# A gated pair of 2-D spectral filters on one core: folded transforms, 32-row inverse tiles, column 0 by a permutation matmul, the exchange through DRAM, last sums on GpSimd

## The chip, the cores and the metric

One core of one Trainium2 chip. The metric is the device time of one execution in microseconds, as the median of several. The profile covers one execution. Its span (first to last instruction) is 1.7 to 2.7 us shorter than the time of the same run. A run counts as slow when it is over 1.5% above the fastest of its kernel; verdicts use the others, the fast ones.

Some terms. In the views PE is TensorE's matmuls, PEld its weight loads, DVE is VectorE, ACT ScalarE, POOL GpSimd, and SP the queue of SyncE, which issues transfers. Matmuls write to the memory PSUM, and an eviction is the copy of a finished tile from there to the memory SBUF, where the next matmul reads it. The granted clock is PE's clock as a share of full speed. The DMA share is the mean busy share of the core's 16 DMA engines. A line such as L275 is a line of kernel.py. "Start to start" is the time from the start of one instruction to the start of the next on the same engine.

## The reference

```python
x = A_x                                     # (1, 2048, 1024) bf16
g = sigmoid((x * gate_w).sum(-1, keepdims=True))
a = irfft2(rfft2(x) * (A_w_r + 1j * A_w_i)) # over S = 2048 and D = 1024
b = irfft2(rfft2(x) * (B_w_r + 1j * B_w_i))
return g * a + (1 - g) * b
```

Both filters see the same x, so the forward transform is shared. The products differ, and the gate mixes the two on the way back.

## The kernel before

All transforms are matmuls with constant matrices. Row s is split as s2 (128) x s1 (16). A forward pass runs over s2 (`f1`), over d (`f2`) and over s1 (`f3`); then comes the complex product with both weights (`cmul`); the inverse runs over s1 (`i1`), over s2 with the gate's mix (`i2`) and over d (`i3`). Even and odd frequencies of d are separate ("par"). Each has 8 units of 256 rows, so 16 units in all. Between `i1` and `i2` the rows must change places, which is the exchange.

```python
def f2(n):                                   # over d: contraction of 512, output 512
    for tt in range(2):
        for q in range(4):
            nc.tensor.matmul(ps[:, tt*512:(tt+1)*512], lhsT=y[:, q, par, 2*t:2*t+2],
                             rhs=FD[:, par, q, :], start=(q == 0), stop=(q == 3))
    nc.scalar.copy(out=T, in_=ps)            # every eviction of the units is on ScalarE
...
def cmul(n):                                 # four products and two sums, all on DVE
    for r in range(2):
        nc.vector.tensor_tensor(p[r], xb[r], w, ALU.mult)       # 2048 elements
    nc.vector.tensor_tensor(Y[:, 0], p1[..., 0], p2[..., 1], ALU.subtract)   # 1024
    nc.vector.tensor_tensor(Y[:, 1], p1[..., 1], p2[..., 0], ALU.add)
...
def i1(n, r):                                # 64 x 64 tiles, two accumulating matmuls
    for k in range(2):
        for tt in range(2):
            for jh in range(2):
                nc.tensor.matmul(ps[hp(jh), tt*512:(tt+1)*512], lhsT=WI[hp(jh ^ tt), 2*u+tt, w, :],
                                 rhs=Y[hp(jh ^ tt), k, 2*tt:2*tt+2, o:o+256], ...)
    nc.scalar.copy(out=rl[:, :, r, :], in_=ps)
    if r == 1:                               # the exchange, SBUF to SBUF
        nc.gpsimd.dma_start(RR[par][p0:p0+29:4, :, :], rl[:, tt])
...
def gate_hat():                              # row sums of the gate, then turned by a DMA
    nc.scalar.copy(out=zs, in_=ps)           # (patterns cut) it writes single elements 16 apart
    nc.scalar.dma_start(zt, zs[0:97:32])
...
def i3(par, v):                              # over d, back: 4 matmuls of 512 columns per row
    for ch in range(4):
        nc.tensor.matmul(ps[:, s*512:(s+1)*512], lhsT=V[:, s, ch, :], rhs=IG[:, par*4+ch, :], ...)
    # even: copied to SBUF; odd: out = even + odd, even - odd, on DVE
```

## Time and profile before

| | before |
|---|---|
| time, median (range) | 146.72 us (146.09 to 148.42) |
| profiled span | 144.4 us |
| mean granted clock of PE | 0.96 |
| DMA traffic | 29.2 MB |

The first line of the profile's page gives busy time of each engine, its share of the span and its instructions:

```profile
PE 121.9 (84%) x1188; PEld 68.1 (47%) x1206; DVE 97.6 (68%) x113; ACT 93.3 (65%) x97; POOL 19.6 (14%) x37
```

No engine fills the span. The views by stage, which the prediction reads, show why: the bound moves from PE to ScalarE (ACT) and back. To read this kernel, use start-to-start intervals rather than printed durations, since neighbours overlap.

### The profile page before, as it was taken

To read this page: it belongs to the slowest core of one execution; us is meant where nothing else is said; L and a number is where in the kernel's file an instruction comes from. 1 tells how busy PE (TensorE), PEld (TensorE's weight loads), DVE (VectorE), ACT (ScalarE), POOL (GpSimd) and SP (SyncE) were. 2 spreads that over 40 slices of the span, in tenths; PEclk is the share of its full clock that TensorE was granted. 3 is DMA by queue.
4 is the path that set the end of the run, shared out by engine and by line. 5 is a ranking of instruction groups with operands and counts; after the bars stand their busy time and mean duration, and the time that the engine had idled before them with its cause. 6 is when DMAs were issued, how large, how long until landed. Compare 5 with 4: busy or idle time off the path is not lost.

```text
span 144.4 us, 2878 instructions
## 1 busy us (share of the span) xinstructions
PE 121.9 (84%) x1188; PEld 68.1 (47%) x1206; DVE 97.6 (68%) x113; ACT 93.3 (65%) x97; POOL 19.6 (14%) x37
## 2 busy tenths in 40 slices
PE   6999979929899898888867999868869999999910
PEld 2688844416344443334324345433455665756500
DVE  0177740089279999999999279599433456898990
ACT  4255546665699999999995899997935244253200
POOL 1000000000033222233333033033330000000000
PEclk9999999975799999999999999999999999999985
DMA  4999999968716999999865315527464000464553
GB/s 148 298 361 419 406 411 405 415 244 284 297 14 168 240 279 278 353 250 202 163 139 133 126 18 140 131 43 168 110 166 110 0 0 0 167 253 166 208 228 145
DMA packets 11088, 29.19 MB, mean 202 GB/s; under 512 B 3781, under 2 KB 4165, under 8 KB 10949
## 3 DMA queue, kind: packets, MB, share of 16 engines
q1 hardware_dynamic: 6048, 20.55, 38.3%
q0 software_dynamic: 4608, 8.41, 24.8%
q8 instruction: 9, 0.15, 0.5%
q10 hardware_dynamic: 420, 0.07, 0.3%
q14 instruction: 3, 0.02, 0.0%
HBM read 16.42 MB, written 4.19 MB: 143 GB/s over the span
## 4 chain that ended last, share of the span: by engine, by line
PE 55%; ACT 24%; DMA 9%; issue 4%; DVE 2%; another core or an unknown queue 2%; DVEq 1%; POOL 0%; ACTq 0%; POOLq 0%
PE pt L378 18%; PE pt L218 10%; PE pt L275 10%; ACT rl L349 10%; PE pv L367 9%; DMA re<-rl 5%; DMA zt<-zs 4%; ACT X L310 4%; ACT T L279 3%; PE pt L344 3%; ACT V L370 2%; PE pt L155 2%; ACT zs L245 2%; DVE ot L390 2%
## 5 line engine op out<-in xcount | busy, mean ns | idle before, releaser
L275 PE MATMUL pt<-fd,y 128*128 128x512 bf16 x117 | 30.5, 394 | 3.8 <-ACT rl L349 2.6
L349 ACT CAST rl<-pt 128x1024 bf16<-128x1024 f32 x32 | 32.9, 1038 | 0.0
L378 PE MATMUL pt<-ig,V 128*128 128x512 bf16 x121 | 29.6, 379 | 1.1 <-ACT V L370 0.7
L370 ACT CAST V<-pv 128x1024 bf16<-128x1024 f32 x16 | 16.3, 1021 | 19.2 <-PE pv L367 19.2
L344 PE MATMUL pt<-Y,wi 64*64 64x512 bf16 x256 | 20.1, 387 | 3.8 <-ACT T L279 0.8
L275 PEld LDWEIGHTS <-y 128*128 128x128 bf16 x128 | 12.6, 100 | 20.3 <-issue 8.6
L279 ACT CAST T<-pt 128x1024 bf16<-128x1024 f32 x16 | 16.3, 1017 | 8.3 <-PE pt L275 4.1
L378 PEld LDWEIGHTS <-V 128*128 128x128 bf16 x128 | 11.7, 98 | 13.9 <-ACT V L370 1.9
L354 POOL DMA_DIRECT2D re<-rl x16 | 9.6, 606 | 59.8 <-ACT rl L349 59.8
L310 ACT CAST X<-pt 128x1024 bf16<-128x1024 f32 x16 | 16.5, 1033 | 0.0
L218 PE MATMUL pt<-f_84,re 128*128 128x256 bf16 x128 | 15.6, 289 | 0.0
L218 PEld LDWEIGHTS <-re 128*128 128x128 bf16 x128 | 13.0, 103 | 3.1 <-DMA re<-in_x_dram 0.8
L228 ACT CAST y<-pt 128x1024 bf16<-128x1024 f32 x8 | 8.1, 1013 | 8.4 <-PE pt L218 8.4
L354 POOL DMA_DIRECT2D ro<-rl x16 | 9.5, 596 | 26.4 <-ACT rl L349 26.4
L386 DVE COPY re<-pt 128x1024 f32<-128x1024 f32 x5 | 6.1, 1225 | 10.2 <-PE pt L378 10.2
L226 DVE CAST y<-pt 128x1024 bf16<-128x1024 f32 x7 | 8.6, 1225 | 5.2 <-PE pt L218 5.2
L344 PEld LDWEIGHTS <-wi 64*64 64x64 bf16 x256 | 6.4, 106 | 11.9 <-issue 10.7
L389 DVE TENSOR_TENSOR ot<-pt,re 128x1024 bf16<-128x1024 f32 x8 | 9.8, 1224 | 3.0 <-PE pt L378 3.0
L367 PE MATMUL pv<-ea,re 128*128 128x128 bf16 x64 | 8.1, 219 | 2.9 <-DMA re<-rl 1.7
L295 PE MATMUL pt<-T,wf 64*64 64x512 bf16 (+2 forms) x192 | 9.8, 307 | 0.4 <-ACT T L279 0.3
L367 PEld LDWEIGHTS <-re 128*128 128x128 bf16 x128 | 7.5, 98 | 5.4 <-issue 2.5
L390 DVE TENSOR_TENSOR ot<-re,pt 128x1024 bf16<-128x1024 f32 x8 | 9.7, 1210 | 0.0
(96 smaller groups left out, 128.2 us busy)
## 6 DMA issues: line engine op xcount, KB each, us to landing
re<-rl POOLq DMA_DIRECT2D x16, 256.0 KB, 8.0
ro<-rl POOLq DMA_DIRECT2D x16, 256.0 KB, 5.1
out_dram<-ot SPq DMA_DIRECT2D x8, 512.0 KB, 2.6
re<-in_x_dram SPq DMA_DIRECT2D x7, 512.0 KB, 8.6
ro<-in_we_dram SPq DMA_DIRECT2D x4, 516.0 KB, 8.0
y<-in_wo_dram SPq DMA_DIRECT2D x4, 512.0 KB, 6.5
fd<-cst_fd SPq DMA_DIRECT2D x2, 512.0 KB, 9.1
ig<-cst_ig SPq DMA_DIRECT2D x1, 1024.0 KB
```

The source lines that it names most:

```text
L218: nc.tensor.matmul(ps[:, q * 256:(q + 1) * 256], lhsT=x[:, s1, h * 512 + q * 128:h * 512 + (q + 1) * 128], rhs=(bc(F1[:, 0, :]).to_broadca ...
L275: nc.tensor.matmul(ps[:, tt * 512:(tt + 1) * 512], lhsT=y[:, q, par, 2 * t:2 * t + 2, :, :].rearrange("p j s c -> p (j s c)"), rhs=FD[:, p ...
L279: nc.scalar.copy(out=T[:].rearrange("p a b -> p (a b)"), in_=ps[:])
L295: nc.tensor.matmul(ps[ho, tt * 512 + dst:tt * 512 + dst + ln], lhsT=WF[hp(jh), 2 * u + tt, w, :], rhs=T[hp(jh), tt, src:src + ln], start=( ...
L310: nc.scalar.copy(out=xo, in_=ps[:].rearrange("p (t r m) -> p t r m", t=2, r=2))
L344: nc.tensor.matmul(ps[hp(jh), tt * 512:(tt + 1) * 512], lhsT=WI[hin, 2 * u + tt, w, :], rhs=Y[hin, k, 2 * tt:2 * tt + 2, o:o + 256], start ...
L349: nc.scalar.copy(out=rl[:, :, r, :], in_=ps[:].rearrange("p (t m) -> p t m", t=2))
L354: nc.gpsimd.dma_start(RR[par][p0:p0 + 29:4, :, :], rl[:, tt].rearrange("p r m -> p (r m)"))
L367: nc.tensor.matmul(ps[:, s * 512 + ch * 128:s * 512 + ch * 128 + 128], lhsT=RR[par][:, s1, c0 + 256 * ab:c0 + 256 * ab + 128], rhs=Ew[:, s ...
L370: nc.scalar.copy(out=V[:].rearrange("p s c k -> p (s c k)"), in_=ps[:])
L378: nc.tensor.matmul(ps[:, s * 512:(s + 1) * 512], lhsT=V[:, s, ch, :], rhs=IG[:, par * 4 + ch, :], start=(ch == 0), stop=(ch == 3))
L390: nc.vector.tensor_tensor(ot[:, :, 1, :], ev, pv, ALU.subtract)
```

## The change

Nearly everything is rewritten to the same mathematics. The intent is to take work from PE and DVE at once.

- d is reordered on the host so that an element and its mirror are added and subtracted right after `f1`. A cosine half then needs only the sums, a sine half only the differences. `f2` has half the columns, and so has part of `i3`.
- `i1` uses 32-row tiles and accumulates all four products in PSUM, so the two DVE sums of `cmul` go.
- Column 0 (and 512), whose two real spectra share one complex column, are split by a permutation matmul and a small DVE patch.
- The exchange goes through DRAM.
- The gate is turned by one-row matmuls.
- GpSimd takes a part of the fold and of the last sums.
- A long list of tokens fixes the order of all engines, on eight single PSUM banks. A token is a step's name with its arguments, and the engine as D, P or A where there is a choice. `U` and `C` are the last stage for one row with 512 and with 256 columns (`i3`, `i3f`), `E` and `EX` copy its result, `EQ` adds the halves of an even row, `OR`, `QD` and `QP` are sums of odd rows, `Y`, `NA` and `N` treat column 0, `GT` and `GK` turn the gate.

```diff
 def f2(n, tt, k):
-        for q in range(4):
-            nc.tensor.matmul(ps[:, tt * 512:(tt + 1) * 512], ... rhs=FD[:, par, q, :], ...)
+        for v in range(2):
+            for b in range(2):
+                nc.tensor.matmul(ps[:, v * 256:v * 256 + 256], ... rhs=C["FD"][:, par, v, b, :], ...)
...
+    def fold(e, s1, par, a, b):
+        for v, op in enumerate((ALU.add, ALU.subtract)):
+            Q[e].tensor_tensor(yo[:, v, k:k + n, s1, :], a..., b..., op)
...
-        nc.vector.tensor_tensor(Y[:, 0, :, 0:M], p1[:, :, 0, 0:M], p2[:, :, 1, 0:M], ALU.subtract)
-        nc.vector.tensor_tensor(Y[:, 1, :, 0:M], p1[:, :, 1, 0:M], p2[:, :, 0, 0:M], ALU.add)
...
+        for q, (w, ri, wi) in enumerate(((0, 0, 0), (64, 1, 1), (128, 0, 1), (128, 1, 0))):
+            for tt in range(2):
+                for H in range(2):
+                    for j in range(2):
+                        r = slice(64 * H + 32 * j, 64 * H + 32 * j + 32)
+                        nc.tensor.matmul(o, lhsT=C["WJ"][r, 2 * u + tt, w:w + 64], rhs=src[r, ri, wi, tt],
+                                         start=(q == 0), stop=(q == 3))
...
-                nc.gpsimd.dma_start(RR[par][p0:p0 + 29:4, :, :], rl[:, tt]...)
+        Q[q].dma_start(SC[n // NU][a:a + 2].rearrange("a p m -> p a m"), RLs[n][:, tt])
+        Q[q].dma_start((Re, Ro)[par][:, v * 2048:v * 2048 + 2048],
+                       SC[par][:].rearrange("a (h v q) m -> (a h) v (q m)", h=4, v=8)[:, v])
...
-        nc.scalar.dma_start(zt[:], zs[0:97:32].rearrange("p t c s -> p (t c s)"))
+                nc.tensor.matmul(ps[32 * j:32 * j + 32, s1:s1 + 1], lhsT=TM["zs"][r, s1, :], rhs=C["one"][r, :], ...)
...
+            rh = bc(g[:, 0:256]).to_broadcast([P, 2, 256]) if ch < 2 else g[:, 256:768]   # i3: 512 columns, no sums
+            nc.tensor.matmul(ps[:, o:o + 256], lhsT=..., rhs=g[:, o:o + 256], ...)        # i3f: 256 columns, sums later
...
+        Q[e].tensor_tensor(EV[:, v, s, 256 * h:256 * h + 256], t[:, 0], t[:, 1], (ALU.add, ALU.subtract)[h])
```

## The prediction

> **What bounds the kernel now.** I read the page's header first: PE is busy 84% of the span, DVE 68%, ACT 65%, so no engine explains the time alone. So I cut the span into stages and asked for each engine's busy time in each. The columns are the stretch in us and its length, then busy us of each engine with its number of instructions, the granted clock, the DMA share and GB/s.
>
> ```profile
> 4.00:20.00 16.00, 15.43 (x128) 12.84 (x126) 8.99 (x10) 8.49 (x9) 0.00 (x0) 1.00 1.01 378
> 20.00:37.00 17.00, 13.65 (x117) 6.75 (x120) 8.16 (x11) 9.15 (x9) 0.00 (x0) 0.82 0.89 345
> 37.00:70.00 33.00, 28.86 (x352) 13.56 (x357) 28.83 (x37) 30.87 (x33) 9.13 (x16) 0.99 0.85 226
> 70.00:97.00 27.00, 22.81 (x250) 10.89 (x248) 20.96 (x27) 24.29 (x27) 6.41 (x11) 1.00 0.45 108
> 97.00:138.00 41.00, 38.37 (x345) 23.16 (x352) 27.67 (x28) 18.98 (x20) 3.55 (x6) 1.00 0.39 127
> ```
>
> The reader is to see three regimes. The first transform (4 to 20) and the last stages (97 to 138) are PE-bound. The middle (37 to 97) is bound by ACT, with DVE and PE close behind. The second stretch is bound by none of them: its clock is 0.82 and PE idles. The chain of waits in order of time (start, length, what) says why:
>
> ```profile
> 23.94 2.35 ACT zs L245
> 26.32 5.80 DMA zt<-zs
> 32.16 1.05 PE pt L254 x8
> 33.23 1.94 ACT g L256 x2
> 35.17 2.31 another core or an unknown queue
> ```
>
> The gate's row sums are turned through a 4 KB DMA of 5.8 us, and ACT's sigmoid stands, in program order, ahead of the evictions. For the middle regime the timeline of ACT shows one unit of 16:
>
> ```profile
> 49.42 1.01 ACT L279 CAST T<-pt 128x1024 bf16<-128x1024 f32 x1 [0.20 <-remote]
> 50.33 1.02 ACT L349 CAST rl<-pt 128x1024 bf16<-128x1024 f32 x1
> 51.23 1.04 ACT L310 CAST X<-pt 128x1024 bf16<-128x1024 f32 x1
> 52.14 1.04 ACT L349 CAST rl<-pt 128x1024 bf16<-128x1024 f32 x1
> 53.38 1.01 ACT L279 CAST T<-pt 128x1024 bf16<-128x1024 f32 x1 [0.20 <-PE pt L275]
> ```
>
> A unit repeats every 3.96 us. Four 1024-wide evictions follow each other at 0.905 us (start to start; the printed 1.02 overlaps), 3.6 us, and the rest is a wait for PE. DVE does 1.155 + 1.155 (products) + 0.61 + 0.61 (sums) + about 0.2, nearly 3.7, in the same period. I use such start-to-start intervals throughout: ACT 0.905 / 0.48 / 0.265 us for 1024 / 512 / 256 elements out of PSUM, DVE 1.10 / 0.57 / 0.30. The 512 and 256 values are estimates: the measured 1024 interval, less 0.853 (ACT) or 1.067 (DVE) as the part that scales with size.
>
> Last, the groups of PE (operand shapes, count, busy us, mean ns):
>
> ```profile
> L275 PE MATMUL pt<-fd,y 128*128 128x512 bf16 x117 | 30.5, 394 | 3.8 <-ACT rl L349 2.6 <-ACT y L224 0.7
> L378 PE MATMUL pt<-ig,V 128*128 128x512 bf16 x121 | 29.6, 379 | 1.1 <-ACT V L370 0.7
> L344 PE MATMUL pt<-Y,wi 64*64 64x512 bf16 x256 | 20.1, 387 | 3.8 <-ACT T L279 0.8 <-DVE Y L330 0.7 <-issue 0.4
> L218 PE MATMUL pt<-f_84,re 128*128 128x256 bf16 x128 | 15.6, 289 | 0.0
> ```
>
> Two groups of 128 full-width matmuls are 60 of PE's 122 us: the transform over d forward (L275) and back (L378). In the chain, eight of L378 take 1.73 us, so 0.216 us each, and sixteen of 128 columns (L367) take 0.89, so 0.056 each.
>
> **What the Trainium skill says.** "TensorE: Matmul & The Clock Gate", section "Back-to-back issue gap": N/2.4 + 2.5 ns a matmul, 216 ns at 512 columns and 56 at 128. The trace agrees exactly (0.216, 0.056), so PE work may be counted in columns. "TensorEngine Tiling (Array Packing)", section "Available Configurations", lists 64x64 as 4 independent tiles and 32x64 as 8. The trace confirms the first: in L344 and L295 four matmuls start 3 to 4 ns apart and the next four about 0.21 us later. Of the second no run here shows anything yet. "GPSIMD Engine Reference", section 3.1, has an fp32 tensor_tensor of 2048 at 4497 ns, about 2.2 ns an element; the kernel before has no such instruction. "DMA: Bandwidth & Descriptors", Specifications, asks for transfers of 512 B or more; the new exchange moves runs of 1 KB in and 4 KB out.
>
> **The change, part by part.**
>
> 1. Folded d, forward. d and its mirror are added and subtracted first, so each cosine or sine half needs half the contraction: 128 matmuls of 256 columns in place of 128 of 512. PE: 128 x 0.216 = 27.6 falls to 128 x 0.11 = 14.1, so minus 13.5 us. The first stage keeps its columns (256 of 128 for 128 of 256, still 14.3 us). The price is the fold itself: before, 16 plain evictions of 1024; now 21 ACT copies of 256 and 8 of 512, 48 DVE sums of 256 from PSUM (14.4 us) and 16 on GpSimd. DVE had about 9 us here, so plus 6.
> 2. Folded d, backward. Of 32 last-stage groups, 20 use 256 columns (80 x 0.11 = 8.8) and 12 keep 512 (48 x 0.216 = 10.4): 19.2 in place of 27.6, minus 8.4 us of PE. The missing sums go to GpSimd: 24 of 256 and 10 of 512, an estimate of 24 x 0.6 + 10 x 1.15 = 26 us from the skill's rate, beside other work.
> 3. 32-row tiles. The complex product's sums (2 x 0.61 a unit, 19.5 us of DVE) move into PSUM accumulation. 512 matmuls of K=32 replace 256 of K=64. At eight at once that is still 64 groups of 0.216 = 13.8 us; at only four at once it would be 27.6.
> 4. Column 0. The 64 one-column matmuls and 8 small copies go; 27 matmuls of 1 to 4 columns and 16 DVE instructions of about 0.16 us come: near even, and DVE gains nothing from it.
> 5. Gate. 64 tiny matmuls do the turn that the DMA did. Of the stretch from 20 to 37, in which PE was busy 13.65 of 17 us at a reduced clock, I expect 4 us back.
> 6. Exchange: SBUF to SBUF on GpSimd's queue becomes 32 stores and 16 loads through DRAM on SP. It is 8.4 MB more traffic, at a mean of 202 GB/s now, with busy slices above 400. The order puts some 9 us of PE work between the last odd store and its first reader; a store lands in 2.6 us now, and a load of 512 KB in 4 to 8 under load.
>
> Counting every instruction of the new order at these intervals gives PE 93 us (before, the same way, 111), DVE 92, ACT 82, GpSimd 39. DVE's parts: products 37, fold 15, last-stage sums 17, evictions 17, the rest 6.
>
> Then by stage, taking the busiest engine (PE, DVE, ACT): first transform 16.4 (PE); units 0 to 3 with the gate and the rest of the odd fold 16.6 (DVE, PE 16.1); to unit 8 9.6 (ACT); to unit 12 15.7 (DVE); the last units with the first inverse work 1.7 + 12.3 + 9.4 (PE, ACT, ACT); even inverse 4.4 (PE); odd inverse 7.9 (PE) and 13.1 (DVE). The sum is 107. Add 3.8 before the first transform, 3.7 from the last DVE instruction to the end (140.7 to 144.4 now), and 2.3, the timed median (146.7) over the profiled span (144.4): 117. For the kernel before, the same sum (15.4, 13.7, 30.9, 24.3, 38.4, plus 4, 6.4 and 2.3) is 135 against 146.7, some 6 of the gap being the gate; outside the gate's stretch the busiest engine fills 90 to 96%. I take 3 to 4 us of loss, since the new order mixes the engines finely and uses eight single PSUM banks rather than three double ones: **121 us**.
>
> **The rivals.** (a) Eight tiles don't run at once: PE gains 14 us in the units, becomes their bound, and the time is 130 to 134. For it: 512 pairs of small instructions; against it, 64x64 tiles start 3 to 4 ns apart, so eight need 28 ns of the 216. I give it one in eight. (b) DVE becomes the bound: 92 us in many short instructions with PSUM waits, and GpSimd adds beside it that may slow it or be slower than the rate read; then the last 25 us stretch by 4 to 8 and the time is 125 to 129. One in five. (c) The exchange through DRAM stalls PE between the even and odd inverse, or stores queue behind loads on SP: 3 to 5 us; small, since even inverse work covers it. (d) The order overlaps stages better than my sum of maxima, which is no lower bound: PE's 93 + 3.8 + 6 + 2.3 = 105 is. Then 113 to 117.
>
> **Range and chances.** 115 to 129 holds (b), (c) and most of (d); (a) lies outside. Even (a) is well below 146.7, so faster by over 2% is near certain; a fault in several parts at once is needed for less.
>
> **What would show it.** Right: the stage of the inverse tiles shows eight starts within 30 ns and about 0.9 us for 32; the forward d matmuls 0.11 us each; PE's plain clock stays 1.0 through 20 to 37; DVE and ACT both above 70% of the span. Wrong: the 32-row group taking 1.7 us a unit (a); DVE instructions longer while GpSimd runs, or the chain's tail full of GpSimd (b); PE waiting for a load of the exchange (c). An error in the total of more than 8 us means the losses between stages, the term I measured least, were mis-sized.

## The result

| | before | changed |
|---|---|---|
| time, median (range) | 146.41 us (145.92 to 148.42) | 119.47 us (119.08 to 119.84) |
| profiled span | 144.4 us | 118.1 us |
| mean granted clock of PE | 0.96 | 1.00 |
| DMA traffic | 29.2 MB | 36.8 MB |

The ratio of fast runs is 0.821 (95% interval 0.816 to 0.827). The time lies 1.5 us under the predicted 121 and well inside 115 to 129.

The page's first line of the changed kernel, and below it the same table of stretches as the prediction shows (stretch and length, busy us of PE, weight loads, DVE, ACT, GpSimd, then clock, DMA share, GB/s):

```profile
PE 102.6 (87%) x1619; PEld 70.4 (60%) x1619; DVE 98.2 (83%) x161; ACT 87.8 (74%) x144; POOL 44.8 (38%) x70
```

```profile
4.00:20.00 16.00, 14.80 (x241) 13.87 (x240) 12.63 (x38) 9.19 (x25) 10.74 (x19) 1.00 1.05 371
20.00:37.00 17.00, 16.76 (x349) 10.75 (x350) 16.71 (x30) 16.70 (x30) 3.22 (x10) 1.00 0.88 331
37.00:70.00 33.00, 28.25 (x521) 16.51 (x520) 31.34 (x42) 31.28 (x41) 0.00 (x0) 1.00 0.92 307
70.00:97.00 27.00, 25.93 (x382) 18.96 (x380) 19.79 (x26) 22.41 (x37) 16.97 (x23) 1.00 0.98 360
97.00:114.00 17.00, 14.00 (x135) 9.27 (x132) 16.45 (x26) 6.75 (x12) 13.27 (x12) 1.00 0.60 220
```

The reader is to see that 20 to 37, which had been the stretch of a dipped clock and an idle PE, now has PE, DVE and ACT all busy for 16.7 of 17 us. From 37 to 70, DVE and ACT are both at 31.3 of 33. From 70 to 97 PE is full, and from 97 on DVE is. Busy time of DVE barely changed (97.6 to 98.2). What changed is that it is spread over the whole span, and that PE has 19 us less to do.

The groups of PE that answer to those shown of before:

```profile
L536 PE MATMUL ps<-p,wj 32*64 32x512 bf16 x512 | 20.3, 381 | 3.7 <-ACT X L203 2.0
L449 PE MATMUL ps<-fd,y 128*128 128x256 bf16 x128 | 17.7, 274 | 0.3 <-ACT rl L203 0.3
L333 PE MATMUL ps<-f,re 128*128 128x128 bf16 x256 | 15.5, 221 | 1.2 <-DMA re<-in_x_dram 1.2
L580 PE MATMUL ps<-ig,V 128*128 128x512 bf16 x48 | 12.0, 380 | 1.4 <-ACT V L203 1.4
L589 PE MATMUL ps<-ig,V 128*128 128x256 bf16 x80 | 11.0, 273 | 0.2 <-ACT V L203 0.2
```

Forward d fell from 30.5 to 17.7 us busy, and backward d from 29.6 to 23.0. The 512 matmuls of 32 rows take what 256 of 64 rows took (20.3 against 20.1), with twice the accumulation. Their starts in the trace show the eight tiles at once: in one unit (at 45.29 us) eight begin within 25 ns, the next eights begin 215, 430 and 645 ns later, and the following 128-row matmul begins 1.00 us after the first. Four more units are like it (215 or 240 ns to the second eight); in most others the second four begin later, after a wait.

The chain of waits of the changed kernel (start, length, what) in the gate's stretch has PE work where the 5.8 us DMA and the sigmoid had stood. One ScalarE eviction of 1.02 us (rl, at 32.47) is among the pieces left out:

```profile
29.01 0.29 PE ps L420 x32
29.30 0.56 PE ps L479 x12
29.86 0.54 PE ps L449 x4
...
34.71 0.45 PE ps L429 x8
35.15 1.27 PE ps L536 x32
36.42 0.54 PE ps L449 x4
36.96 0.56 PE ps L479 x12
```

L420 is the turn by one-row matmuls. It costs 0.29 us for 32 of them.

### The profile page after: what moved, and what is told of

Read it like the earlier page. It is cut to its first block, busy times and chain, and to the rows that moved or that the text cites. A ratio compares the mean times of both kernels' runs of the same rounds, so it can differ in the third digit from the quotient of the medians.

```text
span 118.1 us, 3959 instructions
## 1 busy us (share of the span) xinstructions
PE 102.6 (87%) x1619; PEld 70.4 (60%) x1619; DVE 98.2 (83%) x161; ACT 87.8 (74%) x144; POOL 44.8 (38%) x70
## 4 chain that ended last, share of the span: by engine, by line
PE 48%; DMA 18%; DVE 15%; ACT 8%; issue 5%; SPq 3%; DVEq 1%; ACTq 0%
PE ps L564 9%; DMA re<-in_x_dram 9%; PE ps L449 9%; PE ps L580 7%; DMA re<-sc 6%; PE ps L589 5%; PE ps L333 5%; PE ps L536 5%; DVE p L493 5%; PE ps L479 4%; DVE ot L634 4%; ACT X L203 3%; ACT rl L203 3%; DMA f<-cst_f 2%; DVE rl L205 2%
## 5 line engine op out<-in xcount | busy, mean ns | idle before, releaser
L614 POOL TENSOR_TENSOR re<-wx 128x256 f32<-128x256 f32 x24 | 17.9, 788 | 56.3 <-ACT wx L203 48.9
L203 ACT CAST rl<-ps 128x1024 bf16<-128x1024 f32 x25 | 25.1, 1067 | 0.4 <-PE ps L536 0.3
L203 ACT COPY wx<-ps 128x512 f32<-128x512 f32 (+1 forms) x42 | 18.3, 500 | 8.4 <-PE ps L333 7.4
L536 PE MATMUL ps<-p,wj 32*64 32x512 bf16 x512 | 20.3, 381 | 3.7 <-ACT X L203 2.0
L493 DVE TENSOR_TENSOR p<-X,ro 128x2048 bf16<-128x2048 bf16 x16 | 19.1, 1218 | 0.7 <-ACT X L203 0.5
L203 ACT CAST X<-ps 128x1024 bf16<-128x1024 f32 x16 | 16.9, 1078 | 1.6 <-DVE np L513 1.0
L449 PE MATMUL ps<-fd,y 128*128 128x256 bf16 x128 | 17.7, 274 | 0.3 <-ACT rl L203 0.3
L381 DVE TENSOR_TENSOR y<-ps,wx 128x256 bf16<-128x256 f32 x48 | 16.2, 413 | 0.9 <-ACT wx L203 0.9
L333 PE MATMUL ps<-f,re 128*128 128x128 bf16 x256 | 15.5, 221 | 1.2 <-DMA re<-in_x_dram 1.2
L203 ACT CAST T<-ps 128x512 bf16<-128x512 f32 x26 | 15.8, 676 | 0.0
```

The lines of the kernel that those rows point to most:

```text
L203: nc.scalar.copy(out=out, in_=in_)
L333: nc.tensor.matmul(o, lhsT=lh, rhs=rh, start=(h == 0), stop=(h == 1))
L381: Q[e].tensor_tensor(yo[:, v, k:k + n, s1, :], a.rearrange("p (k c) -> p k c", c=4), b.rearrange("p (k c) -> p k c", c=4), op)
L449: nc.tensor.matmul(ps[:, v * 256:v * 256 + 256], lhsT=y[:, v, par, b, 2 * t:2 * t + 2, :, :].rearrange("p j s c -> p (j s c)"), rhs=C["FD" ...
L493: nc.vector.tensor_tensor(p[:, r], xb, w, ALU.mult)
L536: nc.tensor.matmul(o, lhsT=lh, rhs=src[r, ri, wi, tt], start=(q == 0), stop=(q == 3))
```

## The experiments

Twelve kernels ran, in three groups of four. Each group shares its runs of the kernel before. Ten undo, double or take away a part; a_direct_p and a_qp2p try one change each to the exchange and the end. The theory is the prediction's: after 20 us PE, DVE and ACT are all close to full, so each part given back costs about its engine time in the stretches where that engine is full. The main rivals are that one engine alone bounds the kernel (PE, or ACT and DVE), that the DMA bounds it, and that GpSimd's sums hold the end. Differences from the changed kernel are against its 119.5 us, so across groups. The third group (a_half, a_half_nocol0, a_direct_p, a_qp2p) ran on another chip than the first two, and the fastest run of the kernel before was 143.86 us there and 145.61 in the others, so 1 us across groups shows nothing.

| run | what | time, median us (range) | ratio to before |
|---|---|---|---|
| b_peturn | before, gate turned by matmuls | 143.57 (142.19 to 146.31) | 0.979 |
| a_dvesum | product sums back on DVE | 139.03 (138.85 to 139.99) | 0.952 |
| a_f2x2 | forward d done twice | 128.36 (127.97 to 128.53) | 0.877 |
| a_full_even | backward fold undone, even rows but pairs 2 and 6 | 122.47 (121.65 to 122.72) | 0.837 |
| a_full_odd | the same, row pairs 2 and 6, even and odd | 121.28 (120.56 to 121.51) | 0.829 |
| a_nocol0 | no column 0 (wrong) | 119.20 (118.86 to 120.26) | 0.816 |
| a_gatedma | gate turned by the DMA | 124.50 (122.57 to 126.42) | none given |
| a_direct | exchange SBUF to SBUF, SP queue | 205.16 (203.43 to 206.04) | 1.399 |
| a_direct_p | the same, GpSimd queue, rows spread | 144.54 (142.44 to 147.08) | 0.985 |
| a_half | half of each exchange load (wrong) | 119.32 (119.23 to 119.39) | 0.824 |
| a_half_nocol0 | a_half and a_nocol0 together (wrong) | 118.50 (116.98 to 118.88) | 0.812 |
| a_qp2p | one half sum from DVE to GpSimd | 118.30 (117.29 to 120.82) | 0.814 |

The medians are of all runs. Where some were slow, the medians of the fast ones are: b_peturn 143.39 (3 of 4), a_gatedma 122.57 (1 of 4), a_direct_p 142.65 (2 of 4), a_half_nocol0 117.57 (2 of 4), a_qp2p 117.87 (4 of 6). The profiles of the last four are of slow runs.

### The gate's turn alone, on the kernel before

```diff
-        nc.scalar.dma_start(zt[:], zs[0:97:32].rearrange("p t c s -> p (t c s)"))
+        nc.tensor.matmul(ps[32*j:32*j+32, s1:s1+1], lhsT=zs[r, s1, :], rhs=one[r, :], ...)   # 64 of them
+        nc.scalar.copy(out=zt[:], in_=ps[:, 0:NS1])
```

> The kernel before, with one part of the change alone: the gate's row sums are turned by 64 one-row matmuls and a small ScalarE copy instead of the 5.8 us DMA. Theory (the DMA held ScalarE's sigmoid, which held the evictions, while the clock fell to half): 4 to 6 us less than before, 140 to 142.5 us, and no clock dip between 30 and 38 us. Rival (the weight loads that end the same stretch hold the units anyway, so the wait moves to them): within 1.5 us of before.

It took 143.57 us against 146.52, ratio 0.979 with an interval from 0.968 to 0.989: some 3 us, a little under what was expected. The stretch that had shown PE at 13.65 us and a clock of 0.82:

```profile
20.00:37.00 17.00, 15.71 (x232) 7.73 (x235) 9.17 (x13) 11.73 (x15) 0.00 (x0) 1.00 0.97 375
```

PE gained 2.1 us here and the clock stays at 1.00. The edit also replaced ScalarE's copy of the row sums, which wrote single elements 16 apart and took 2.34 us, by one that writes runs of four (0.59), and it took the issue of the DMA (1.08 us) off ScalarE. So the run shows that the turn held this stretch, but not how much of the 3 us was the transfer and how much ScalarE's own work.

### The complex product's sums back on DVE

```diff
+    nc.vector.tensor_tensor(p00, p00, p11, ALU.subtract)     # 1024 elements, in place, two a unit
+    nc.vector.tensor_tensor(p01, p01, p10, ALU.add)
-    for q, (w, ri, wi) in enumerate(((0, 0, 0), (64, 1, 1), (128, 0, 1), (128, 1, 0))):
+    for q, (w, ri, wi) in enumerate(((0, 0, 0), (128, 0, 1))):
```

> The changed kernel with the complex product's sums given back to DVE (two more adds a unit, 16 x 2 x 0.61 = 19.5 us) and only two of the four accumulating products left on PE (16 x 0.43 = 6.9 us less). Theory (DVE is full from 20 to 70 us, PE has slack there): 10 to 16 us slower, 130 to 136 us. Rival (PE bounds the units): 0 to 4 us faster than the changed kernel's 119.5.

139.03 us: 19.6 us slower, beyond the range expected and equal to the whole 19.5 us of added DVE work, though PE was relieved of half of these matmuls. The stretch from 37 to 70 of this run:

```profile
37.00:70.00 33.00, 22.46 (x269) 11.18 (x269) 32.27 (x48) 23.78 (x29) 0.00 (x0) 0.78 0.68 219
```

DVE is busy 32.3 of 33 us and everything else waits for it. PE falls to 22.5 us, and its granted clock to 0.78. DVE is as full in the stretches on both sides (16.6 of 17 us in 20 to 37, 26.6 of 27 in 70 to 97), so PE's lower clock does not explain the loss. The evictions of T and rl that DVE took over stayed with it in this run; the room for them came from accumulating the products on PE. It is the largest single part among the arithmetic changes.

### Forward d done twice

```diff
-        for v in range(2):
+        for v in (0, 1, 0, 1):
             for b in range(2):
                 nc.tensor.matmul(ps[:, v * 256:v * 256 + 256], ...)
```

> The changed kernel with every forward d matmul done twice, which gives PE back the columns that the forward fold saved (128 x 0.11 = 14 us) and touches nothing else; the result stays right. Theory (PE is full in 20 to 37 and from 70 on, and has about 5 us of slack in 37 to 70): 7 to 11 us slower, 126.5 to 130.5. Rival (ScalarE and DVE bound the units, so PE work there hides): up to 3 us slower.

128.36 us, 8.9 slower, inside the range. Two stretches of this run:

```profile
20.00:37.00 17.00, 17.00 (x304) 12.40 (x310) 12.59 (x26) 13.32 (x24) 3.23 (x10) 1.00 0.75 291
37.00:70.00 33.00, 31.43 (x559) 21.04 (x543) 29.20 (x39) 29.38 (x37) 0.00 (x0) 1.00 0.81 261
```

Of 14 us of added PE work, 9 showed and 5 hid. PE's busy time in these two stretches rose by 3.4 us, most of it in the slack of the middle. So the forward fold is worth about 9 us in this order, and neither PE nor DVE alone bounds the units.

### The backward fold undone, in two parts

```diff
- C:0:v:s  EX:v:s  EQ:v:s:0:P  EQ:v:s:1:P        # even, v not 2 or 6: 256 columns, GpSimd adds
+ U:0:v:s  E:v:s                                 # 512 columns, a plain copy
- C:par:v:s  QD:v:s:h  QP:v:h:g:P or D           # row pairs 2 and 6, even and odd
+ U:par:v:s  OR:v:s:h
```

> The changed kernel with the backward fold undone in the even half: 12 of 16 groups go back to 512 columns (48 x 0.106 = 5.1 us more PE), ScalarE copies finished sums and GpSimd's 24 adds (18.9 us busy) go. Theory (PE bounds 70 to 97 us, GpSimd lies beside it): 3 to 5 us slower, 122.5 to 124.5. Rival (GpSimd's adds hold the end or slow DVE): same or up to 2 us faster, 117.5 to 119.5.

> The changed kernel with the backward fold undone for row pairs 2 and 6 alone: 8 groups go to 512 columns (32 x 0.106 = 3.4 us more PE, half of it after 97 us), and the eight half adds on GpSimd (6 of 1.28 us) and DVE (2 of 1.4 us, one held 2.0 us beside GpSimd) go. Theory (from 97 us on DVE is the full engine, 16.45 of 17 us, and PE has 3 us of slack): 0.5 to 2 us faster, 117.5 to 119. Rival (PE bounds the end too): 1 to 2 us slower.

The even rows cost 3.0 us, as expected: PE bounds 70 to 97, and GpSimd's 24 adds lie beside it. For row pairs 2 and 6 the theory missed. It foresaw 0.5 to 2 us of gain, and the run was 1.8 us slower, as its rival said. Its last stretch shows why:

```profile
97.00:114.00 17.00, 15.95 (x145) 9.93 (x142) 14.89 (x25) 7.28 (x14) 6.39 (x7) 1.00 0.54 198
```

DVE lost 1.6 us of work here and PE gained 2, to 15.95 of 17, and PE became the bound. The end of the changed kernel is balanced between the two engines, so one can't be relieved at the other's cost.

### Column 0 taken away, and the DMA as a bound

```diff
- Y:n  NA:n  N:n                                  # all of them, a_nocol0 and a_half_nocol0
- dma(R[:, v*2048 : v*2048+2048], SC[...][:, v])          # a_half and a_half_nocol0
+ dma(R[:, v*2048 : v*2048+1024], SC[...][:, v, 0:1024])
```

> The changed kernel without the treatment of column 0 (27 small matmuls, 16 small DVE instructions, 3.2 us of DVE); the result is wrong on purpose. Theory (DVE and ScalarE full between 20 and 60 us): 1.5 to 3 us faster. Rival (small instructions fall in gaps): within 0.7 us.

> The changed kernel with only half of each exchange load (4.2 MB less read, the result wrong on purpose, every instruction of the engines unchanged). Theory (from 50 to 97 us the DMA share is 1.0, yet PE waits for a load only about 1 us, so DMA is just behind the engines): 0.3 to 1.5 us faster than 119.5. Rival (DMA is the bound of that stretch): 3 us or more faster. Second rival (fully hidden): no change.

> Both at once: half of each exchange load, and no treatment of column 0 (wrong on purpose). Taking column 0 away alone changed nothing (119.2), and PE then waited 2.2 us for exchange loads instead of 1.0. Theory (its gain was turned into a wait for the DMA): 1.5 to 3 us faster than the half-load run alone. Rival (the small instructions fall in gaps): the same as the half-load run within 0.5.

Without column 0 the time was 119.2: the theory's 1.5 to 3 us did not come, although DVE instructions of 3.2 us in sum had gone. They overlap their neighbours: DVE's busy time fell by only 2.2 us (98.2 to 96.0). The wait of PE's weight loads for the exchange rose from 1.0 to 2.2 us. That suggested that the gain had become a wait for DMA, whose share is near 1.0 from 50 to 97 us. Halving the loads alone changed nothing (119.3), though its DMA share fell from 0.98 to 0.62:

```profile
70.00:97.00 27.00, 25.93 (x383) 18.99 (x382) 19.93 (x27) 22.01 (x38) 17.48 (x24) 1.00 0.62 206
```

PE is busy the same 25.93 us. So the DMA engines, busy with the exchange, are hidden in the changed kernel, and a full DMA row is not a bound by itself. The run says nothing of the first 20 us: the DMA share is 1.05 there, and the chain of the changed kernel is the load of x from 4.12 to 14.76 us before it is PE's. That the DMA bounds this stage was not tested. Both changes together gave 116.98 and 118.15 us in the two fast runs and 118.85 and 118.88 in the two slow. The fast two are 1.2 to 2.3 us under a_half, of the same group, so it leans to the theory, but the spread is as large as the effect. Whether the missing gain of a_nocol0 went into the DMA wait stays open.

### The gate's turn by DMA, in the changed kernel

```diff
- GT:... (64 one-row matmuls)  GK:A (copy)
+ nc.scalar.dma_start(zt, zs[0:97:32])            # right after the copy of the row sums
```

> The changed kernel with the gate's row sums turned by the 4 KB DMA again, as in the kernel before (its copy with the transposed order too), at the places that the new order gives. Theory (the turn's DMA takes 5 to 8 us while the order has the gate's matmuls some 6 to 8 us later): 1 to 4 us slower. Rival (the order leaves enough room, so the gain of part 5 came from the order and not from the matmuls): within 0.7 us.

122.57 us in the one fast run and 124.4 to 126.4 in the three slow: at least 3 us slower, so the rival falls. But the reason given was wrong. The chain of this run (of a slow one, 124.43 us):

```profile
27.24 0.73 ACT wn L280
27.97 0.48 ACT T L203
28.45 2.25 ACT eb L203
30.70 0.02 issue
30.72 1.11 ACTq L413
31.83 0.04 issue
31.87 0.59 ACT T L203
```

In this order the transfer's latency is not in the chain. The copy in the order that the DMA needs, single elements 16 apart, takes ScalarE 2.25 us of the chain and 2.53 in all (the one of the changed kernel, in runs of four, takes 0.78), and ScalarE spends 1.1 us more on issuing the transfer, in a stretch where it is full in the changed kernel (16.7 of 17 us).

### The exchange without DRAM

```diff
-    Q[q].dma_start(SC[...][a:a+2]..., RLs[n][:, tt])     # 32 stores, then 16 loads
+    for j in range(2):                                   # 64 transfers of 128 KB
+        dma(R[4*(a+j) : 4*(a+j)+4, :] as (4, 32, 512), RLs[n][:, tt, j, :])   # a_direct, on SP
+        dma(R[p0+16*j : p0+16*j+13 : 4, :] ..., ...)                          # a_direct_p, on GpSimd
```

> The changed kernel with the exchange SBUF to SBUF again, on the same queue: 64 transfers of 128 KB straight into the rows that the inverse reads, in place of 32 stores and 16 loads through DRAM. 8.4 MB less traffic. Theory (the exchange is hidden either way, since the order leaves 9 us of PE work between the last store and the first reader): within 1.5 us of 119.5. Rival (the DMA engines, 98% busy in 70 to 97, hold something): 1.5 to 4 us faster. Second rival (each direct transfer writes only 4 partitions and is slow): over 2 us slower, with PE waiting for these transfers at its first inverse matmuls.

> The changed kernel with the exchange SBUF to SBUF on GpSimd's queue and with rows spread in steps of four, as the kernel before had it, in 64 transfers of 128 KB (the direct form on SP took 205 us at a DMA share of 0.2 to 0.4). Theory (that loss came from few of the 16 DMA engines carrying a transfer issued by SP, not from SBUF to SBUF as such): under 130 us, with a DMA share above 0.5 between 40 and 90 us, and with less traffic perhaps 1 us better than 119.5. Rival (writing a few partitions at a time is slow from any queue): over 150 us.

The first was 205 us: the second rival held, with a loss far beyond the 2 us it named. The second was 142.65 in its fast runs, a miss for the theory (under 130) and for its rival (over 150). Both were correct. The stretch from 37 to 70, first on SP, then on GpSimd (the latter from a slow run, 147.08 us):

```profile
37.00:70.00 33.00, 15.32 (x264) 9.25 (x264) 17.71 (x27) 14.63 (x19) 0.00 (x0) 0.79 0.44 79
```

```profile
37.00:70.00 33.00, 24.61 (x420) 14.44 (x427) 25.49 (x37) 25.70 (x34) 17.77 (x26) 0.90 0.75 175
```

On SP only 79 GB/s move, at a DMA share of 0.44, and the engines starve. A transfer with four destination rows seems to use few of the 16 DMA engines; that is an inference from the share, not a reading of single engines. On GpSimd the share is higher, but the transfers land after 7.4 to 8.7 us (the stores to DRAM after 4.5), and the waits of that run name what this does:

```profile
POOL re L550 <- DMA re<-rl: 14.1, 7, 4.0
ACT rl L202 <- DMA re<-rl: 10.2, 3, 5.0
```

GpSimd waits 14.1 us for its own earlier transfers before it can issue the next, and ScalarE 10.2 us for an rl buffer that a transfer still reads. Queue and row pattern were changed together between the two runs, so how much each did stays open. The kernel before moved the same rows directly, in 32 transfers of 256 KB to eight rows with runs of 2 KB. PE waited for them 1.7 us and its weight loads 2.2. Neither run used that form, because the new unit layout sends the halves of a unit to rows that lie apart.

### One half sum moved to GpSimd

```diff
- QP:2:1:1:D
+ QP:2:1:1:P
```

> The changed kernel with one of DVE's two half sums of the last stage (row pair 2, which took 2.0 us while GpSimd ran the same operation, against 0.85 for the other) given to GpSimd. Theory (DVE is the full engine after 97 us and PE waited 1.3 us for it at 107; GpSimd then has a 2.6 us gap that absorbs 1.3): 0.8 to 2 us faster, 117.5 to 118.7. Rival (PE or the stores hold the end, as undoing the odd half, 1.8 us slower, suggests): within 0.4 us of 119.5.

The reason lies in the timelines of DVE and then GpSimd in the changed kernel (start, length, what):

```profile
102.57 1.99 DVE L646 TENSOR_TENSOR ot<-pq 128x512 bf16<-128x512 f32 x1
...
112.94 0.85 DVE L646 TENSOR_TENSOR ot<-pq 128x512 bf16<-128x512 f32 x1
```

```profile
100.26 3.75 POOL L646 TENSOR_TENSOR ot<-pq 128x512 bf16<-128x512 f32 x3
```

The same DVE add takes 1.99 us when GpSimd does its own adds for most of that time, and 0.85 when it hardly does. With it moved, the median was 118.3, and the four fast runs of six were 117.29 to 118.57. The ratio 0.814 has an interval from 0.802 to 0.826, which covers that of the changed kernel (0.816 to 0.827). It is probably about 1% better than the changed kernel, which these rounds do not establish.

## Why the prediction was right

The prediction set the order's stages end to end. The same stages, read off the starts of their first matmuls in the trace, in us from the start of the span:

| point of the order | predicted | measured |
|---|---|---|
| first d matmul | 20.2 | 19.4 |
| unit 4, second half | 36.8 | 34.1 |
| unit 8 | 46.4 | 43.3 |
| unit 12 | 62.1 | 59.8 |
| first odd inverse | 89.9 | 90.6 |
| odd row pair 4 | 97.8 | 98.5 |
| end of the last DVE instruction | 110.9 | 115.0 |
| end of the span | 114.6 | 118.1 |

The order splits unit 4: its first half starts at 28.4 us already. The row takes the second half.

1. **Forward fold.** Right: 128 matmuls at 0.11 us. Giving the columns back cost 8.9 us, less than their 14, as the slack of the middle said. One reading of the skill was incomplete. "TensorE: Matmul & The Clock Gate", section "Back-to-back issue gap", gives N/2.4 + 2.5 ns for a single, isolated matmul, and for a stream of weight loads and matmuls other times (131 ns at 512 columns, 81 at 128). The streams of this trace take 216 and 56 ns, so it was the trace that made the count by columns right.
2. **Backward fold.** Right in kind: the even rows are worth 3.0 us, row pairs 2 and 6 1.8. GpSimd was mis-sized a little: 0.79 us where 0.6 was taken, 1.28 where 1.15 was taken. It lay beside other work all the same.
3. **32-row tiles.** Right: eight at once, and the DVE sums are worth their full 19.5 us in this order. Rival (a) fell. The estimate of 0.86 us a unit was 1.00. The 64-row tiles of `f3` take 0.56 in the chain where 0.43 was taken from before. The 0.13 us in each place comes where tile shapes change: before, the same twelve matmuls of `f3` stood between groups of their own shape and took 0.434 us in the trace, and in the changed kernel four 128-row matmuls between two such groups take 0.54 where 4 x 0.11 is 0.44. "TensorEngine Tiling (Array Packing)", section "Key Properties", says that a change of the tiling mode drains TensorE, and gives no figure; these runs show the cost without isolating it. A weight load that is not hidden at the change would fit as well: one of 128 columns takes 0.10 us, and the first of the new shape starts only about 0.2 us after the last matmuls of the old (62.47 after 62.26 us).
4. **Column 0.** Right as far as tested: taking it away gained 0.3 us. The kernel before's form of it was not timed.
5. **Gate.** Right in direction, some 3 us in place of 4 on the kernel before. The working blamed the transfer's 5.8 us; the runs show ScalarE's copy of single elements and the issue beside it, and in the changed kernel, where undoing it costs 3 us or more, it is these that stand in the chain. The sum for the kernel before put "some 6" of its gap of 11.7 us on the gate; its own table leaves 17.0 - 13.65 = 3.35 in that stretch, and the run gave some 3.
6. **Exchange.** Right that it is hidden, and that little PE time waits for it (1.0 us). Its sizes were off a little: stores landed after 4.5 us where 2.6 was taken, and all traffic rose by 7.6 MB, not 8.4. It understated what the form does: the two direct forms tried cost 23 (fast runs) and 86 us. That the way through DRAM is cheap because of its patterns is argued, not shown. The 512 B that the prediction cites was not tested, as every form here has runs of 1 KB or more.
7. **Losses between stages.** 3 to 4 us were allowed over the sum of 117, and about 2.5 came. That the total came so near was partly luck, as errors of opposite sign cancelled. They lay elsewhere than thought: the gate's stretch was 1.9 us shorter than its sum, from unit 4 to the odd inverse 3.4 longer, and the last stage 3.4 longer than DVE's 13.1. Part of the last is rival (b): the add of 1.99 us, counted as 0.57. Another part is a misreading. The prediction took 1.10 us for 1024 elements out of PSUM on DVE, but the kernel before shows 1.14 start to start (L389 to L390), and the changed kernel 1.14, 0.60 and 0.33 us for 1024, 512 and 256 elements where 1.10, 0.57 and 0.30 were taken. ScalarE's intervals were right (0.90, 0.48, 0.26). In the last stage 22 PSUM adds and the two SBUF adds (1.91 and 0.82 us start to start) make some 2.3 of the 3.4 us, and DVE's idle time 0.5. "GPSIMD Engine Reference", section 1, names contention with DVE instructions that have two SBUF inputs; the pair of 1.99 and 0.85 us agrees with it, as does the weights' difference (512 bf16 elements), which took 0.83 us once, while GpSimd added, against 0.42 otherwise. The rest of that stage was not taken apart.

The parts measured singly (19.6, 8.9, 3.0, 1.8, at least 3) add up to more than the 27 us gained. That fits a balance: when three engines are full, each part given back alone makes its engine the bound. No run took the new order or the eight single PSUM banks apart from the arithmetic, so what they are worth by themselves stays open.

## What to carry to other kernels

Read a kernel whose busy shares are 65 to 85% by stage, and count the new work in start-to-start intervals from the old trace; the sum of each stage's fullest engine, plus the head, the tail and a few us, was within 2% here, though single stages were off by up to 3.4 us and partly cancelled. Take each interval from instructions that truly follow each other. Moving sums from DVE into PSUM accumulation paid their whole time here, where DVE was full, and PE carried them on 32-row tiles in the busy time that 64-row tiles had taken (20.3 against 20.1 us). Check the shape of a row exchange before its volume: more traffic through DRAM in long runs beat less traffic in transfers of four rows.

## What the Trainium skill lacked or had wrong

- "TensorEngine Tiling (Array Packing)", "Key Properties": no size for the drain at a change of mode. Here groups of 32-row and 64-row tiles take 0.13 to 0.14 us longer than their columns (1.00 against 0.86, 0.56 against 0.43), and four 128-row matmuls between them 0.10 (0.54 against 0.44). That 32x64 gives eight concurrent tiles, which it lists, is confirmed: eight starts within 25 ns, the next eight 215 ns later in two units and 240 in three.
- "TensorE: Matmul & The Clock Gate", section "Back-to-back issue gap": its times for a stream of weight loads and matmuls (131 ns at 512 columns, 81 at 128) don't fit this kernel, where eight of 512 take 1.73 us (216 ns each) and sixteen of 128 take 0.89 (56 ns). Its formula for an isolated matmul does.
- "GPSIMD Engine Reference", section 3.1: for tensor_tensor only a time at 2048 elements and a rate per element, no fixed part. Adds of 256 fp32 take 0.79 us (0.74 in the fold) and of 512 1.28 to 1.29, so some 2 ns an element and about a quarter of a us fixed.
- No page gives a size for a ScalarE copy that writes single bf16 elements 16 apart. Here it takes three to four times the one that writes runs of four (512 elements: 2.34 against 0.59 us in the kernel before and its variant, 2.53 against 0.78 in the changed kernel's variant and the changed kernel).
